# A third score bank for VectorE, and layer 2's FFN spread over the next chunk's attention, in a two-layer transformer kernel

## The chip, the cores and the metric

The kernel runs on one core of one Trainium2 chip. The metric is the device time of one execution in microseconds. The granted clock is the share of TensorE's full clock that the profile records.

## The reference

Two identical layers, each with attention and an FFN, in bfloat16, on one sequence of 2048 rows of 512 columns. There are 32 heads of 16 columns, and the FFN's width is 1792.

```python
x = A_x
for layer in range(2):                       # written out in the reference
    q, k, v = heads(layernorm(x) @ wqkv)     # 32 heads of 16
    p = softmax(q @ k.T / 4)                 # 2048 x 2048 for each head
    x = x + (p @ v) @ wo
    h = gelu(layernorm(x) @ w1 + b1)         # tanh form
    x = x + h @ w2 + b2
```

## The kernel before

A Python scheduler with a clock of its own decides, while the program is built, in which order each engine runs its instructions. Its thread priorities (smaller is more urgent) and conditions are therefore part of the kernel: a changed number reorders the instructions of all engines.

The scores are computed in tiles of 128 keys by 512 queries of one head, each in one PSUM bank. There are 2 x 32 x 16 x 4 = 4096 of them. PSUM's eight banks are laid out so:

```python
SLOTS = ((0, 1, 2), (3, 4))   # the large and the small score slot: exponentials on ScalarE
PVB = 5                       # value products of the running pass (32 columns for each of 4 heads)
MISC = (6, 7)                 # projections, FFN, and spare score tiles for VectorE
DU = 7                        # pattern buffers: 7, in pairs and one half
```

While ScalarE takes the exponential of one slot, PE (TensorE) fills the other. Besides, VectorE takes some tiles and approximates the exponential. It makes a bfloat16 bit pattern with a multiply and an add, and two further passes make three shifted copies. PE then needs four value products for such a tile in place of one, with weighted copies of the values.

```python
def scores(self):
    while True:
        sl = yield ("acq", "s")                  # a free slot
        cells = [...]                            # a tile for each of its banks
        ...
        op = _Op("pe", MM, fns, ...)             # the score matmuls of the slot
        # when the op is placed, tiles for VectorE may be attached in spare banks 7 or 6
        op.late = lambda op, start: self.attach(op, start, cells, extra, free)
        yield op
        for d, b, pair, j in extra:
            yield ("spawn", self.dfirst(pair, j, b), DPRIO)
            if j == 0:
                yield ("spawn", self.dchain(pair), CPRIO)
        ...

def dfirst(self, pair, j, b):                    # VectorE, first pass: from PSUM
    u = self.T["DU"][pair["du"]][:, 0, j, :]
    yield _Op("dve", 0.68, lambda e: e.tensor_scalar(u, self.bank(b), E_SCALE, E_BIAS,
              op0=ALU.mult, op1=ALU.add), reads=["B.%d" % b], writes=[...])
    yield ("rel", "dbank", b)                    # dchain: two more passes for each pair

def exps(self):                                  # ScalarE
    ...
    yield _Op("act", 0.065 + 0.4267 * n, lambda e: e.activation(out=dst, in_=src, func=ACT.Exp, scale=0.25), ...)
    yield ("rel", "s", sl)                       # the slot is free
```

After the last pass of a chunk of 512 queries come the output projection, a layer norm, the FFN and (after layer 1) the projections for layer 2. They run between the attention instructions of the next chunk. `when(l, c, part)` holds a piece back until that share of the next chunk's score tiles is placed.

The softmax here doesn't subtract the row's maximum and nothing guards it: scores larger than these inputs give would overflow.

Of the kernel before, what the change touches and what calls it, by code (L numbers as in the profile page):

```python
# [19 lines left out]
SLOTS = ((0, 1, 2), (3, 4))  # L20
PVB = 5
MISC = (6, 7)
# [5 lines left out]
GP = 2  # L28

DU = 7  # L30
LAST = 450
EARLY = 4
KD = ((4, 5, 6, 7), (0, 1, 2, 12))
NKD = 4
# [5 lines left out]
MID = 1.4  # L40
QUEUE = 4
DPRIO = 9
CPRIO = 16
FPRIO = 1.5
PVP = 2
PTURG = 6
DUURG = 0
BACKLOG = 1.0
DULOW = 1
DWIDE = 2  # L50
RWIDE = 2
# [287 lines left out]
def bass_interleave_layers__mha_block__dense_activation_gelu__prompt_kernel(  # L339
# [15 lines left out]
    with ExitStack() as es:  # L355
# [20 lines left out]
        du = sb([128, DU // 2, 4, 2, 512], U16, "du")  # L376
        T["DU"] = [du[:, i, :, :, :] for i in range(DU // 2)]
        if DU % 2:
# [60 lines left out]
class _Plan:  # L439
# [164 lines left out]
    def projections(self, l, c, prio):  # L604
        T = self.T
        if l == 0:
            def src(dc, t):
                return T["K"][1][:, dc, t * 128:(t + 1) * 128] if t is not None else T["K"][1][:, dc, 512 * c:512 * c + 512]
            skeys = ["XL.%d" % t for t in range(4 * c, 4 * c + 4)]
        else:  # L610
            def src(dc, t):
                return T["XF"][:, dc, (t % 4) * 128:(t % 4) * 128 + 128] if t is not None else T["XF"][:, dc, :]
            skeys = ["XF.%d" % j for j in range(4)]
        ph = self.phase[c]
        units = []
        if l == 1:
            units = [("K", b) for b in range(4)] + [("V", 4 * c + b) for b in range(4)] + [("Q", b) for b in range(4)]
        else:
            for b in range(4):
                units.append(("K", b))  # L620
                if c == 0:
                    units.append(("Q", b))
                units.append(("V", 4 * c + b))
            if c > 0:
                units += [("Q", b) for b in range(4)]
        for j, (kind, i) in enumerate(units):
            p = prio + (0.01 * j if l else 0.5 if kind == "Q" and c > 0 else 0)
            if l:
                yield ("cond", self.when(0, c, 0.52 + 0.024 * j))
            yield ("spawn", self.proj(l, kind, i, c, src, skeys, ph, (kind, l, i, c)), p)  # L630

    def norm(self, l, qc, g, b, part, final):
# [161 lines left out]
    def post(self, l, c):  # L794

        T = self.T
        tiles = range(4 * c, 4 * c + 4)
        yield ("need", ("otn", l, c, 3))
        for t in tiles:
            yield ("spawn", self.wo(l, c, t), 10)  # L800
        for t in tiles:
            yield ("need", ("xready", t, 2 * l + 1))
        self.phase[c] = 2 * l + 1
        xf, xk = lambda t: T["XF"][:, :, (t % 4) * 128:(t % 4) * 128 + 128], lambda t: ["XF.%d" % (t % 4)]
        yield ("spawn", self.ln(c, xf, xk, 11), 11)
        for t in tiles:
            yield ("need", ("lnt", t, 2 * l + 1))
        for p in range(NFC // 2):
            yield ("cond", self.when(l, c, 0.06 + (0.06 if l else 0.055) * p))
            yield ("spawn", self.hpair(l, c, p), 12 + 0.1 * p)  # L810
        if (l, c) != (NL - 1, self.NQ - 1):
            yield ("spawn", self.gelu(l, c), 12)
        for t in tiles:
            yield ("spawn", self.ytile(l, c, t), 13)
        for t in tiles:
            yield ("need", ("xready", t, 2 * l + 2))
        if l == NL - 1:
            return
        self.phase[c] = 2 * l + 2
        yield ("spawn", self.ln(c, xf, xk, 14), 14)  # L820
        for t in tiles:
            yield ("need", ("lnt", t, 2 * l + 2))
        yield from self.projections(l + 1, c, 15)
# [38 lines left out]
    def setup_attention(self):  # L862
        self.pas = self.passes()
        self.alist, self.dlist, self.left, self.pvleft = [], [], [], {}
        self.base, self.span = {}, {}
        n = 0
        for pi, (l, qc, g, kts, part, final) in enumerate(self.pas):
            self.alist.append([(pi, kt, a) for kt in kts if kt not in KD[l] for a in range(4)])
            self.dlist.append([(pi, kt, a) for kt in kts if kt in KD[l] for a in range(4)])
            self.left.append(4 * len(kts))  # L870
            n += 4 * len(kts)
            self.base[(l, qc)] = n
            for a in range(4):
                self.pvleft[(pi, a)] = len(kts)
        self.total, self.scored, self.nd, self.pa, self.pv = n, 0, 0, 0, 0
        for l in range(NL):
            for c in range(self.NQ):
                self.span[(l, c)] = LAST if (l, c) == (0, self.NQ - 1) else 260 if (l, c) == (1, 0) else 512
        self.aq = {k: [] for k in self.pvleft}
        self.dq = {k: [] for k in self.pvleft}  # L880
        self.cap = [2] * (DU // 2) + [1] * (DU % 2) + [2]
        self.lead = [min(pi for pi, p in enumerate(self.pas) if p[0] == l) for l in range(NL)]
        self.duleft, self.open, self.starved, self.lend = {}, None, 0, 2

    def vcopies(self):
# [64 lines left out]
    def take(self, c, free):  # L950
        self.scored += 1
        self.left[c[0]] -= 1
        if self.left[c[0]] == 0:
            free.append(self.s.tokens[("qp", c[0])])

    def attach(self, op, start, cells, extra, free):
        pools = self.s.pools
        used = {c[2] for c in cells}
        if sum(th.op.cost for th in self.s.threads if th.op is not None and th.op.eng == "dve" and th.prio >= 10) > BACKLOG:
            return  # L960
        for home in ("dbank", "misc"):
            for b in list(pools[home]):
                if len(used) == 4 or self.lend == 2 or not (self.open or pools["du"]):
                    return
                if any(self.s.end.get(ev, 0.0) > start + TOL for ev in self.P.deps([], ["B.%d" % b]) if ev[0] != "pe"):
                    continue
                d = self.next_d(used, start)
                if d is None:
                    if self.open:
                        self.open["full"] = True  # L970
                        self.open = None
                    return
                used.add(d[2])
                pools[home].remove(b)
                if self.open is None:
                    self.open = {"du": pools["du"].pop(0), "cells": [], "full": False}
                pair = self.open
                pair["cells"].append(d)
                extra.append((d, b, pair, len(pair["cells"]) - 1))
                if len(pair["cells"]) == self.cap[pair["du"]]:  # L980
                    self.open = None
                f, r = self.score(d, self.s.tokens[("qp", d[0])], b)
                op.fns.append(f)
                op.reads += r
                op.writes.append("B.%d" % b)
                self.take(d, free)
                self.nd += 1

    def scores(self):
        u = 0  # L990
        pools = self.s.pools
        while True:
            sl = yield ("acq", "s")
            cells = []
            for _ in SLOTS[sl]:
                c = self.next_act()
# [6 lines left out]
            fns, reads, writes, free, extra = [], [], [], [], []  # L1003
            for c, b in work:
                l, qc, g = self.pas[c[0]][:3]
                yield ("need", ("qp", c[0]))
                yield ("need", ("K", l, g // 2, c[1] // 4))
                f, r = self.score(c, self.s.tokens[("qp", c[0])], b)
# [1 line left out]
                reads += r  # L1010
                writes.append("B.%d" % b)
                self.take(c, free)
            ahead = 0.065 + 0.4267 * len(SLOTS[1 - sl])
            op = _Op("pe", MM, fns, reads=reads, writes=writes, mode="S", slack=max(SLACK, ahead - LATE))
            op.late = lambda op, start: self.attach(op, start, cells, extra, free)
            yield op
            for d, b, pair, j in extra:
                yield ("spawn", self.dfirst(pair, j, b), DPRIO)
                if j == 0:
                    yield ("spawn", self.dchain(pair), CPRIO)  # L1020
# [11 lines left out]
    def dfirst(self, pair, j, b):  # L1032
        u = self.T["DU"][pair["du"]][:, 0, j, :]
        yield _Op("dve", 0.68, lambda e: e.tensor_scalar(u, self.bank(b), E_SCALE, E_BIAS, op0=ALU.mult, op1=ALU.add),  # L1034
                  reads=["B.%d" % b], writes=["DU.%d.0.%d" % (pair["du"], j)] + self.over(pair["du"]))
        pair["done"] = pair.get("done", 0) + 1
        yield ("rel", "dbank", b)

    def over(self, du):
        return ["K0.%d.%d" % (i, c) for i in (2, 3) for c in range(self.NQ)] if du == len(self.cap) - 1 else []  # L1040
# [46 lines left out]
    def exps(self):  # L1087
        T = self.T
        u = 0
        while True:  # L1090
# [3 lines left out]
            sl, cells = got  # L1094
# [14 lines left out]
            for r, (pi, kt, a) in zip(run, cells):  # L1109
                l, _, g = self.pas[pi][:3]  # L1110
                h = 8 * (g // 2) + 2 * a + (g % 2)
                self.aq[(pi, a)].append((T["V"][l][:, kt, h, 0:17], T["PT"][:, r, :],
                                         ["V%d.%d" % (l, kt), "V%d1" % l, "PT.%d" % r], ("pt", r), True, kt))
            yield ("rel", "s", sl)
            u += 1
        for sl in range(len(SLOTS)):
            yield ("take", ("s", sl))
# [134 lines left out]
```

## Time and profile before

| | |
|---|---|
| median | 1698.77 us (3 runs, 1696.15 to 1699.09; a fourth, later, makes it 1698.42) |
| ScalarE busy | 1597.9 us, 94% |
| VectorE busy | 1251.7 us, 74% |
| PE busy | 1441.1 us, 85% |

The page of the profiled execution. The first line is the span; the second the busy time of each engine; PEclk is the granted TensorE clock in tenths of full speed, in 40 slices (9 is 0.9 or more); the last the shares of the chain of waits.

```profile
span 1700.3 us, 28713 instructions
...
PE 1441.1 (85%) x11935; PEld 370.9 (22%) x11935; DVE 1251.7 (74%) x2377; ACT 1597.9 (94%) x1386; POOL 103.1 (6%) x134
...
PEclk9999999989998999999898999988999899898988
...
ACT 68%; PE 23%; issue 5%; DVE 3%; DMA 1%; POOL 0%; POOLq 0%; SPq 0%
...
```

The groups of instructions, shapes apart: line, engine, operation, shapes and count, then busy time in us and mean ns of one, then the engine's idle time before them and what ended it. The first two lines are the exponentials of the large and of the small slot.

```profile
...
L1106 ACT ACTIVATE pt<-ps 128x1536 bf16<-128x1536 f32 x667 | 1012.3, 1518 | 39.3 <-PE ps L919 25.7 <-PE ps L1165 12.1
L1106 ACT ACTIVATE pt<-ps 128x1024 bf16<-128x1024 f32 x666 | 729.7, 1096 | 6.2 <-PE ps L919 5.4 <-PE ps L1165 0.2
L919 PE MATMUL ps<-qp,kt 32*128 32x512 bf16 x4096 | 549.5, 399 | 175.5 <-ACT pt L1106 152.6 <-DVE du L1034 3.9 <-DVE kt L1034 3.2
...
L1034 DVE TENSOR_SCALAR du<-ps 128x512 uint16<-128x512 f32 x572 | 387.1, 686 | 199.5 <-PE ps L919 192.3 <-PE ps L778 2.3
...
```

Instructions on ScalarE overlap by some 0.15 us, so the mean durations overstate what one costs. The better unit is the time from the end of the predecessor to its own end. In the trace the median of that is 1.344 us for three banks and 0.916 us for two. I call the sum of these units the **exponential work** (667 x 1.344 + 666 x 0.916 + one single bank = 1507.0 us), and everything in which an exponential ends later than that a **stall** (57.1 us). With these two the span closes:

| us, profiled run | before |
|---|---|
| until the first exponential starts | 18.4 |
| exponential work | 1507.0 |
| stalls | 57.1 |
| gelus, table loads, copies between exponentials | 65.8 |
| after the last exponential (the last chunk's FFN) | 52.1 |
| sum | 1700.3 |

Who waited for whom, in total, times and longest in us: ScalarE first, then PE.

```profile
...
ACT pt L1106 <- PE ps L919: 31.0, 55, 2.1
...
ACT pt L1106 <- PE ps L1165: 12.3, 11, 2.7
...
```

```profile
...
PE ps L919 <- ACT pt L1106: 152.6, 305, 1.1
...
PE ps L919 <- DVE du L1034: 3.9, 10, 0.8
...
PE ps L919 <- DVE kt L1034: 3.2, 6, 1.0
...
```

ScalarE waits for score matmuls (L919) and, where no probability buffer is free, for value products (L1165).

### The profile page before, as it was taken

The numbers are of one execution on the slowest core, as the hardware profiler recorded it, in microseconds if no ns is written. First come the engines' busy times: TensorE is split into PE (matmuls) and PEld (weight loads), VectorE is DVE, ScalarE is ACT, GpSimd is POOL, SyncE is SP. The second block draws the span as 40 slices with busy tenths as digits, with TensorE's granted clock in tenths as the row PEclk, the third lists the DMA queues.
The fourth block names the chain that finished last, engine by engine and source line by source line (L and its number), as shares of the span: only waits on it lengthen the run. The fifth ranks groups of instructions, "written<-read, shape, count | busy, mean of one in ns | idle before, by whom it ended". The sixth has DMA issues, their size and how long they took to land.

```text
span 1700.3 us, 28713 instructions
## 1 busy us (share of the span) xinstructions
PE 1441.1 (85%) x11935; PEld 370.9 (22%) x11935; DVE 1251.7 (74%) x2377; ACT 1597.9 (94%) x1386; POOL 103.1 (6%) x134
## 2 busy tenths in 40 slices
PE   7987789888898888899887987789888897898876
PEld 2221122222221222222122221112222221221212
DVE  6478897568885787667776778887678689885861
ACT  6999999999999999999999999998999999999972
POOL 3100010000000000000100010100000000000000
PEclk9999999989998999999898999988999899898988
DMA  6000001001010101101011010001001000110001
GB/s 173 13 1 1 1 13 45 13 20 32 23 41 8 26 26 28 42 1 44 7 38 32 1 44 8 1 13 38 22 23 39 22 11 1 26 38 13 8 13 50
DMA packets 85150, 42.49 MB, mean 25 GB/s; under 512 B 34589, under 2 KB 85022, under 8 KB 85022
## 3 DMA queue, kind: packets, MB, share of 16 engines
q1 hardware_dynamic: 85022, 40.65, 9.0%
q8 instruction: 96, 1.57, 0.4%
q14 instruction: 32, 0.26, 0.1%
HBM read 30.68 MB, written 2.10 MB: 19 GB/s over the span
## 4 chain that ended last, share of the span: by engine, by line
ACT 68%; PE 23%; issue 5%; DVE 3%; DMA 1%; POOL 0%; POOLq 0%; SPq 0%
ACT pt L1106 64%; PE ps L1165 8%; PE ps L919 7%; PE ps L737 3%; ACT g L763 3%; PE ps L776 2%; PE ps L578 2%; DVE du L1034 1%; PE ps L575 1%; DMA xf<-xln 1%; ACT L1106 1%; ACT L763 1%; PE ps L680 1%; DVE du L1059 0%; DVE du L1061 0%
## 5 line engine op out<-in xcount | busy, mean ns | idle before, releaser
L1106 ACT ACTIVATE pt<-ps 128x1536 bf16<-128x1536 f32 (+1 forms) x1334 | 1520.1, 1306 | 45.4 <-PE ps L919 31.0
L919 PE MATMUL ps<-qp,kt 32*128 32x512 bf16 x4096 | 549.5, 399 | 175.5 <-ACT pt L1106 152.6
L1034 DVE TENSOR_SCALAR du<-ps 128x512 uint16<-128x512 f32 x572 | 387.1, 686 | 199.5 <-PE ps L919 192.3
L1165 PE MATMUL ps<-pt,v 128*17 128x512 bf16 x3334 | 468.9, 400 | 5.1 <-DVE xt L653 2.1
L1165 PE MATMUL ps<-du,vc 128*17 128x512 bf16 x1716 | 327.8, 402 | 0.0
L919 PEld LDWEIGHTS ps<-qp,kt 32*128 32x128 bf16 x4096 | 139.7, 91 | 750.2 <-ACT pt L1106 375.3
L1061 DVE TENSOR_SCALAR du<-du 128x2048 uint16<-128x2048 uint16 (+1 forms) x289 | 198.4, 688 | 3.7
L776 PE MATMUL ps<-w,g 128*128 128x512 bf16 x448 | 136.0, 413 | 46.0 <-ACT g L763 46.0
L1165 PE MATMUL ps<-du,v 128*17 128x512 bf16 x572 | 165.0, 403 | 2.6 <-DVE xt L653 1.2
L905 POOL TENSOR_SCALAR qp<-q,mask 128x512 bf16<-128x512 bf16 x84 | 61.3, 730 | 1378.2 <-PE ps L919 1370.1
L737 PE MATMUL ps<-xf,wr 128*128 128x512 bf16 x448 | 123.6, 391 | 15.1 <-DMA xf<-xln 15.0
L1165 PEld LDWEIGHTS ps<-pt,v 128*17 128x17 bf16 x3334 | 89.2, 88 | 164.8 <-issue 136.4
L1059 DVE TENSOR_SCALAR du<-du 128x1024 uint16<-128x1024 uint16 (+1 forms) x289 | 121.7, 423 | 3.8
L1165 PE MATMUL ps<-dh,vc 128*17 128x512 bf16 x300 | 105.7, 413 | 0.0
L1034 DVE TENSOR_SCALAR kt<-ps 128x512 uint16<-128x512 f32 x90 | 61.6, 684 | 39.1 <-PE ps L919 38.5
L1165 PEld LDWEIGHTS ps<-du,vc 128*17 128x17 bf16 x1716 | 73.3, 91 | 68.7 <-issue 45.6
L750 DVE TENSOR_SCALAR g<-ps,hb1t 128x512 bf16<-128x512 f32 x98 | 73.2, 747 | 15.7 <-PE ps L737 14.6
L1034 DVE TENSOR_SCALAR dh<-ps 128x512 uint16<-128x512 f32 x100 | 68.6, 686 | 21.4 <-PE ps L919 20.7
L1165 PE MATMUL ps<-kt,vc 128*17 128x512 bf16 x270 | 71.1, 390 | 0.0
L776 PEld LDWEIGHTS ps<-w,g 128*128 128x128 bf16 x448 | 32.6, 101 | 118.0 <-issue 59.6
L783 DVE TENSOR_TENSOR x<-x,ps 128x512 bf16<-128x512 bf16 x32 | 21.8, 681 | 46.1 <-PE ps L778 38.6
L737 PEld LDWEIGHTS ps<-xf,wr 128*128 128x128 bf16 x448 | 33.4, 99 | 76.6 <-issue 49.6
(70 smaller groups left out, 913.5 us busy)
## 6 DMA issues: line engine op xcount, KB each, us to landing
wr<-in_B_w_dram SPq DMA_DIRECT2D x56, 256.0 KB, 2.8
wr<-in_A_wqkv_dram SPq DMA_DIRECT2D x24, 256.0 KB, 2.7
wr<-in_A_wo_dram SPq DMA_DIRECT2D x16, 256.0 KB, 2.7
x<-in_A_x_dram SPq DMA_DIRECT2D x4, 512.0 KB, 8.9
out_dram<-x SPq DMA_DIRECT2D x16, 128.0 KB, 1.7
w<-in_B_w_dram SPq DMA_DIRECT2D x1, 1792.0 KB, 10.7
g<-in_A_wqkv_dram SPq DMA_DIRECT2D x3, 512.0 KB, 6.5
xf<-xln SPq DMA_TRANSPOSE x48, 2.4
```

What stands on the lines that cost most here:

```text
L578: fns.append(lambda e, dc=dc: e.matmul(pb, lhsT=wt(dc), rhs=src(dc, None), start=(dc == 0), stop=(dc == NDC - 1)))
L737: fns = [lambda e, dc=dc, j=j, pb=pb: e.matmul(pb, lhsT=T["WR"][:, w, 256 * dc + 128 * j:256 * dc + 128 * j + 128], rhs=T["XF"][:, dc, :], ...
L750: yield _Op("dve", 0.74, lambda e, fc=fc, pb=pb: e.tensor_scalar(T["G"][:, fc, :], pb, T["HB1T"][:, fc:fc + 1], None, op0=ALU.add), reads= ...
L763: fns.append(lambda e, g=g: e.activation(out=g, in_=g, func=ACT.Gelu_apprx_tanh))
L776: fns = [lambda e, fc=fc: e.matmul(pb, lhsT=T["G"][:, fc, q], rhs=T["W2"][:, fc, :], start=(fc == 0), stop=False) for fc in range(NFC)]
L905: yield _Op("pool", 0.7, lambda e, s=s, b=b, t=t, qc=qc: e.tensor_scalar(T["QP"][:, s, :], T["Q"][:, b, 512 * qc:512 * qc + 512], T["MASK" ...
L919: return (lambda e: e.matmul(o, lhsT=lhsT, rhs=rhs, start=True, stop=True, tile_position=(32 * a, 0)), ["K%d.%d.%d" % (l, g // 2, kt // 4) ...
L1034: yield _Op("dve", 0.68, lambda e: e.tensor_scalar(u, self.bank(b), E_SCALE, E_BIAS, op0=ALU.mult, op1=ALU.add), reads=["B.%d" % b], write ...
L1059: yield _Op("dve", 0.08 + 0.14 * n, lambda e: e.tensor_scalar(U[:, 1, 0:n, :], U[:, 0, 0:n, :], SHIFT, None, op0=ALU.add), reads=key[0], w ...
L1061: yield _Op("dve", 0.08 + 0.28 * n, lambda e: e.tensor_scalar(U[:, 2:4, 0:n, :], U[:, 0:2, 0:n, :], 2 * SHIFT, None, op0=ALU.add), reads=k ...
L1106: yield _Op("act", 0.065 + 0.4267 * n, lambda e, src=src, dst=dst: e.activation(out=dst, in_=src, func=ACT.Exp, scale=0.25), reads=["B.%d" ...
L1165: op.fns.append(lambda e, o=o, lhsT=lhsT, rhs=rhs, a=a, st=not begun[a], sp=self.pvleft[k] == 0: e.matmul(o, lhsT=lhsT, rhs=rhs, start=st, ...
```

## The change

Its intent is twofold. First, VectorE may also take a tile out of the large slot: when no tile could be attached in a spare bank and VectorE is about free (within `SWAP` = 0.5 us), the slot's third bank gets a VectorE tile, and ScalarE's exponential covers two banks only. The slot becomes free when both engines are done. Second, the FFN of layer 2 is spread over more of the next chunk, and the second FFN matmul (of both layers) and the projections start later in it. Four settings change with it: the priority of layer norms (`LNP`), that of the later VectorE passes (`CPRIO`), the urgency of value products when pattern buffers run out (`DUURG`), and a backlog limit.

```diff
+LNP = 7
+SWAP = 0.5
+HB = (0.05, 0.05)
+HS = (0.05, 0.09)
+YB = (0.4, 0.7)
+YS = (0.05, 0.06)
+JB = 0.64
+JS = 0.025
-CPRIO = 16
+CPRIO = 8
-DUURG = 0
-BACKLOG = 1.0
+DUURG = 1
+BACKLOG = 9
 ...
-                yield ("cond", self.when(0, c, 0.52 + 0.024 * j))       # projections of layer 2
+                yield ("cond", self.when(0, c, JB + JS * j))
 ...
-        yield ("spawn", self.ln(c, xf, xk, 11), 11)                      # the second one was 14
+        yield ("spawn", self.ln(c, xf, xk, LNP), LNP)
 ...
-            yield ("cond", self.when(l, c, 0.06 + (0.06 if l else 0.055) * p))
+            yield ("cond", self.when(l, c, HB[l] + HS[l] * p))
 ...
+            yield ("cond", self.when(l, c, YB[l] + YS[l] * (t % 4)))    # second FFN matmul
             yield ("spawn", self.ytile(l, c, t), 13)
 ...
+    def swap(self, op, start, cells, extra, free):
+        if extra or self.lend == 2 or len(cells) < 3 or not (self.open or self.s.pools["du"]):
+            return
+        if self.s.clock["dve"] > start + SWAP:
+            return
+        ...                                  # the slot's third tile goes back to its queue,
+        self.join(op, d, SLOTS[0][2], extra, free)   # a tile for VectorE takes the bank
 ...
-            ahead = 0.065 + 0.4267 * len(SLOTS[1 - sl])
+            ahead = 0.065 + 0.4267 * self.held[1 - sl]
-            op.late = lambda op, start: self.attach(op, start, cells, extra, free)
+            op.late = lambda op, start: (self.attach(op, start, cells, extra, free), self.swap(op, start, cells, extra, free))
 ...
-            yield ("rel", "s", sl)
+            yield from self.slot_done(sl)    # both users must be done
```

## The prediction

> **What bounds it now.** ScalarE. The page's busy line gives ACT 94% of the span (1598 us), VectorE 74%, PE 85%; the chain of waits is 64% exponentials (L1106). Between 18 and 1648 us ACT runs 667 three-bank and 666 two-bank exponentials nearly back to back. In the trace one ends 1.344 us (three banks) or 0.916 us (two) after its predecessor: 0.428 us a bank and 0.06 us an instruction. Together they need 1507 us; about 57 us more are stalls, 48 of them before a three-bank exponential, when PE had only a short two-bank one in which to refill the large slot. ACT's waits agree (PE scores 31 us; value products, which hold the probability buffers, 12 us). Seven gelus with table loads cost 62 us. The first 18 us and the last 52 us (the last chunk's FFN) are fixed.
>
> **What the change does.** From the instruction order of both programs:
> - VectorE takes 838 score tiles instead of 762. The exponentials become 530 three-bank and 834 two-bank: 712 + 764 = 1476 us, 31 us less. About 137 third banks go over; some 60 ordinary attachments to spare banks are lost, so 76 tiles are net.
> - VectorE: 76 first passes (0.686 us) and their share of the two later passes (1.12 us a pair): about 95 us more, 1252 to about 1345 us, 80% of the shorter span.
> - PE: 228 more value products, in fours 57 rounds of 0.21 us, 12 us. PE has that slack on average.
> - Places with four or more dense matmuls between score groups fall from 165 to 115. At 1100-1200 us, early in layer 2, where ACT stalled about 10 us, there should be less pile-up. Layer 2's last gelu comes later, 139 instead of 226 ScalarE tiles before the end, still in front of the tail.
> - Scores, gelus, table loads and dense matmuls keep their counts.
>
> **On the critical path.** All 31 us are ACT work. Against that: (a) a swapped large slot has a two-bank exponential too, so PE has 0.92 us, not 1.34, to refill the small slot behind it. Applying before's mean stall for each kind of PE work between score groups to the new order, I estimate 62 us of stalls instead of 57. (b) The large slot now needs ACT and VectorE both to finish. VectorE's queue is in order and fuller; where an operation waiting for PE stands ahead, the slot is held and ACT starves: a few us. (c) The smoother FFN returns a few us. Simultaneous reads are of different banks, which the Trainium skill, "PSUM — Partial Sum Buffer", section "PSUM bank collisions raise a hardware error", says run clean; no run here tests it yet.
>
> Net gain about 26 us: **1672 us**, 8 in 10 between 1658 and 1688. Faster by over 2%: 0.25; within 2%: 0.74; slower by over 2%: 0.01.
>
> **What would show it.** Exponential busy time (1520 us) falls to about 1490; VectorE busy about 1340 us; PE's waits for ACT before scores fall, its waits for VectorE's first passes rise from 8 us to 10-25; ACT's waits for PE scores stay at 25-45 us; the tail stays near 52 us; granted clock near 0.93.
>
> **What would make it wrong.** VectorE lagging behind the schedule's assumption: then PE waits tens of us for first passes and the gain vanishes. Layer 2's stalls shrinking by more than (a) and (b) cost: then 1655-1662 us. A denser PE stream lowering the granted clock, value products falling behind: ACT's wait for them well over 12 us.

## More of the kernel before

One run of the kernel before, at 1918.26 us with a mean granted clock of 0.641, was slow. It left no trace and its cause is open.

PE waits for ScalarE much more (152.6 us) than ScalarE for PE. That made PE look as if it had room. The next view shows what this reading misses. It gives, for stretches of the span, the busy us and the instruction counts of each engine, and the granted clock:

```profile
...
core 0: us, PE busy (x) PEld busy (x) DVE busy (x) ACT busy (x) POOL busy (x), PEclk, DMA share, GB/s
658.00:664.00 6.00, 3.90 (x39) 0.90 (x33) 5.58 (x14) 6.00 (x7) 0.01 (x1) 0.98 0.13 26
664.00:667.40 3.40, 3.40 (x29) 0.72 (x27) 0.60 (x1) 2.59 (x3) 0.00 (x0) 0.54 0.19 38
667.40:670.80 3.40, 1.78 (x20) 0.55 (x17) 3.29 (x9) 3.40 (x4) 0.00 (x0) 0.96 0.33 67
670.80:674.20 3.40, 3.40 (x30) 0.66 (x29) 1.42 (x3) 2.50 (x3) 0.00 (x0) 0.53 0.06 13
674.20:690.00 15.80, 15.41 (x127) 4.11 (x120) 13.79 (x26) 15.73 (x15) 0.69 (x1) 1.00 0.12 34
...
```

In the second and fourth stretch, one 3.4 us window each, the clock is near one half. PE is busy from end to end and ScalarE is busy only 2.59 and 2.50 of 3.40 us. In the stretches at full clock ScalarE is busy nearly throughout.

## The result, and the profile after

In the first comparison the changed kernel took 1679.13 us (median of 4 runs, 1676.37 to 1683.28) against 1698.42 us (4 runs), a ratio of 0.9891 with a 95% interval of 0.9867 to 0.9914. Ratios here are the mean time of one kernel's fast runs over that of the other's of the same rounds, so they are not quite the ratio of the medians that I quote. It is 1.1% faster, clear of noise.

The page, the groups and the waits of the changed kernel, the lines that answer to those of before:

```profile
span 1678.4 us, 29283 instructions
...
PE 1440.2 (86%) x12013; PEld 376.7 (22%) x12163; DVE 1322.5 (79%) x2543; ACT 1571.8 (94%) x1416; POOL 108.9 (6%) x134
...
PEclk9999999999999999989989999889899989799898
...
ACT 53%; PE 36%; issue 7%; DVE 4%; DMA 1%; POOL 0%; POOLq 0%; SPq 0%
...
```

```profile
...
L1154 ACT ACTIVATE pt<-ps 128x1024 bf16<-128x1024 f32 x834 | 854.6, 1078 | 17.9 <-PE ps L930 14.5 <-PE ps L1213 2.1
L1154 ACT ACTIVATE pt<-ps 128x1536 bf16<-128x1536 f32 x530 | 795.6, 1501 | 32.4 <-PE ps L930 18.5 <-PE ps L1213 12.3
L930 PE MATMUL ps<-qp,kt 32*128 32x512 bf16 x4096 | 555.4, 397 | 147.6 <-ACT pt L1154 121.9 <-DVE du L1074 5.5 <-DVE mv L519 2.3
...
L1074 DVE TENSOR_SCALAR du<-ps 128x512 uint16<-128x512 f32 x626 | 424.4, 685 | 161.3 <-PE ps L930 154.8
...
```

```profile
...
ACT pt L1154 <- PE ps L930: 32.9, 71, 1.4
...
ACT pt L1154 <- PE ps L1213: 14.4, 12, 6.0
...
```

```profile
...
PE ps L930 <- ACT pt L1154: 121.9, 239, 8.1
...
PE ps L930 <- DVE du L1074: 5.5, 14, 0.9
...
PE ps L930 <- DVE kt L1074: 1.0, 2, 0.8
...
```

The exponentials shift from three banks to two (530 and 834), as the order of the program had said, and their busy time falls from 1520.1 to 1493.9 us. ScalarE still waits as much for PE as before. PE hardly waits for VectorE's first passes (L1074): 5.5 + 1.0 us here against 3.9 + 3.2 us. The account closes again:

| us, profiled runs | before | changed | difference |
|---|---|---|---|
| until the first exponential starts | 18.4 | 19.3 | +0.9 |
| exponential work | 1507.0 | 1476.3 | -30.7 |
| stalls | 57.1 | 66.5 | +9.4 |
| gelus, table loads, copies | 65.8 | 65.8 | 0 |
| after the last exponential | 52.1 | 50.4 | -1.7 |
| sum | 1700.3 | 1678.4 | -21.9 |

So the work went as foreseen, and a third of it came back as stalls. To see whose stalls they are, I took every stalled exponential. I asked which came last for it: a free probability buffer, or the score matmuls of its slot. For the latter, I asked what came last before them: PE's own previous work, ScalarE's release of the slot, or a VectorE pass. The trace has the times of all semaphore updates, so this is a reading of the trace and not of the schedule.

| stalls by what came last, us | before | changed |
|---|---|---|
| PE still in value products | 27.2 | 33.0 |
| PE still in dense matmuls | 16.0 | 14.9 |
| value products late, no probability buffer free | 13.8 | 15.7 |
| ScalarE's release of the slot alone | 0 | 2.0 |
| VectorE's first pass (always of a tile in bank 7) | 0 | 1.0 |
| all | 57.1 | 66.5 |

The largest single stall of the changed kernel is new, 6 us near 1137 us. The timeline there (start us, us, engine, what; in brackets the idle time before it and its releaser):

```profile
...
1125.56 5.54 ACT L1154 ACTIVATE pt<-ps 128x1024 bf16<-128x1024 f32 x5
...
1130.19 0.68 DVE L517 BATCH_NORM_STATS2 stats<-x 128x6 f32<-128x512 bf16 x1
...
1131.21 0.66 DVE L517 BATCH_NORM_STATS2 stats<-x 128x6 f32<-128x512 bf16 x1
...
1132.47 0.66 DVE L517 BATCH_NORM_STATS2 stats<-x 128x6 f32<-128x512 bf16 x1
...
1133.49 0.69 DVE L1109 TENSOR_SCALAR du<-du 128x2048 uint16<-128x2048 uint16 x1
...
1134.71 0.68 DVE L1109 TENSOR_SCALAR du<-du 128x2048 uint16<-128x2048 uint16 x1
1135.31 0.68 DVE L657 TENSOR_TENSOR kt<-kt,ps 128x512 f32<-128x512 f32 x1
...
1136.04 0.12 PEld L1213 LDWEIGHTS ps<-pt,v 128*17 128x17 bf16 x8 [1.70 <-DVE kt L657]
1136.04 1.03 PE L1213 MATMUL ps<-pt,v 128*17 128x512 bf16 x8 [0.78 <-DVE kt L657]
...
1137.13 1.45 ACT L1154 ACTIVATE pt<-ps 128x1536 bf16<-128x1536 f32 x1 [6.03 <-PE ps L1213]
...
```

VectorE runs layer-norm statistics (L517) and later passes (L1109) before it reaches the addition (L657) that frees the value products' bank. PE waits for it, no probability buffer comes free, and ScalarE stands for 6.03 us.

Then there is the clock. In the records of both traces it is either full or one half, and the half-clock spells last multiples of 3.4 us. Those that begin inside the attention (before the last exponential ends) come to 205 us before and 171 us in the changed kernel. (The 184 us in the expectation of e7 counts one more, which begins 10 us after the last exponential.) Of the 57.1 us of stalls before, 38.9 us fall into these spells or the 2 us after them, which are some 16% of the attention; of the changed kernel's 66.5 us, 38.2 us do. So the stalls at full clock rose, from 18.2 to 28.3 us, and those of the half clock stayed about the same. (Two stalls of before, 3.0 us, lie at the very edge of the 2 us; with them the split is 41.9 and 15.2 us.)

What precedes a spell is a window in which PE had less to do. (A window is one stretch of 3.41 us on the grid on which all the spells begin and end.) Before, the 35 such windows had 16.4 matmul starts on average and PE busy for 50% of the time, the other full-clock windows 26.8 starts and 89%. Nearly all of PE's idle time in them, 55.5 of 60 us, ended with a result of ScalarE (exponentials 36.6 us, gelus 18.9 us). The Trainium skill, "TensorE: Matmul & The Clock Gate", section "What's actually happening", says much the same: the slow state is the default, and the clock falls back to it after an idle window of about 3.4 us. This trace agrees on the window and the clock, with spells in multiples of 3.41 us and a clock of 0.5, but most of the windows in front of a spell were not idle: 32 of the 35 had 7 matmul starts or more. There the measurement decides.

### The profile page after: what moved, and what is told of

It reads as the page before. It is cut to its first block, busy times and chain, and to the rows that moved or that the text cites. A ratio compares the mean times of both kernels' runs of the same rounds, so it can differ in the third digit from the quotient of the medians.

```text
span 1678.4 us, 29283 instructions
## 1 busy us (share of the span) xinstructions
PE 1440.2 (86%) x12013; PEld 376.7 (22%) x12163; DVE 1322.5 (79%) x2543; ACT 1571.8 (94%) x1416; POOL 108.9 (6%) x134
## 4 chain that ended last, share of the span: by engine, by line
ACT 53%; PE 36%; issue 7%; DVE 4%; DMA 1%; POOL 0%; POOLq 0%; SPq 0%
ACT pt L1154 50%; PE ps L1213 13%; PE ps L930 11%; PE ps L784 5%; PE ps L745 3%; ACT g L771 2%; PE ps L586 2%; PE ps L583 1%; DVE du L1074 1%; PE ps L688 1%; DVE du L1109 1%; DMA xf<-xln 1%; ACT L771 0%; DVE kt L1074 0%; DVE g L758 0%
## 5 line engine op out<-in xcount | busy, mean ns | idle before, releaser
L1154 ACT ACTIVATE pt<-ps 128x1536 bf16<-128x1536 f32 (+1 forms) x1364 | 1493.9, 1242 | 50.3 <-PE ps L930 32.9
L1074 DVE TENSOR_SCALAR du<-ps 128x512 uint16<-128x512 f32 x626 | 424.4, 685 | 161.3 <-PE ps L930 154.8
L1213 PE MATMUL ps<-du,vc 128*17 128x512 bf16 x1878 | 338.6, 399 | 2.1 <-DVE du L1109 1.1
L1109 DVE TENSOR_SCALAR du<-du 128x2048 uint16<-128x2048 uint16 (+1 forms) x317 | 218.0, 691 | 2.9
L784 PE MATMUL ps<-w,g 128*128 128x512 bf16 x401 | 123.1, 408 | 36.0 <-ACT g L771 29.7
L745 PE MATMUL ps<-xf,wr 128*128 128x512 bf16 x394 | 115.9, 389 | 22.4 <-DMA xf<-xln 13.1
L1107 DVE TENSOR_SCALAR du<-du 128x1024 uint16<-128x1024 uint16 (+1 forms) x317 | 130.2, 417 | 2.7
L1213 PE MATMUL ps<-dh,vc 128*17 128x512 bf16 x339 | 114.3, 395 | 0.0
L1074 DVE TENSOR_SCALAR dh<-ps 128x512 uint16<-128x512 f32 x113 | 77.3, 684 | 29.4 <-PE ps L930 28.2
L1074 DVE TENSOR_SCALAR kt<-ps 128x512 uint16<-128x512 f32 x99 | 67.7, 684 | 32.5 <-PE ps L930 31.5
L1213 PE MATMUL ps<-kt,vc 128*17 128x512 bf16 x297 | 72.3, 405 | 0.0
L1109 DVE TENSOR_SCALAR dh<-dh 128x1024 uint16<-128x1024 uint16 x113 | 47.8, 423 | 1.2
```

What stands on the lines that cost most here:

```text
L745: fns = [lambda e, dc=dc, j=j, pb=pb: e.matmul(pb, lhsT=T["WR"][:, w, 256 * dc + 128 * j:256 * dc + 128 * j + 128], rhs=T["XF"][:, dc, :], ...
L784: fns = [lambda e, fc=fc: e.matmul(pb, lhsT=T["G"][:, fc, q], rhs=T["W2"][:, fc, :], start=(fc == 0), stop=False) for fc in range(NFC)]
L1107: yield _Op("dve", 0.08 + 0.14 * n, lambda e: e.tensor_scalar(U[:, 1, 0:n, :], U[:, 0, 0:n, :], SHIFT, None, op0=ALU.add), reads=key[0], w ...
L1109: yield _Op("dve", 0.08 + 0.28 * n, lambda e: e.tensor_scalar(U[:, 2:4, 0:n, :], U[:, 0:2, 0:n, :], 2 * SHIFT, None, op0=ALU.add), reads=k ...
L1154: yield _Op("act", 0.065 + 0.4267 * n, lambda e, src=src, dst=dst: e.activation(out=dst, in_=src, func=ACT.Exp, scale=0.25), reads=["B.%d" ...
L1213: op.fns.append(lambda e, o=o, lhsT=lhsT, rhs=rhs, a=a, st=not begun[a], sp=self.pvleft[k] == 0: e.matmul(o, lhsT=lhsT, rhs=rhs, start=st, ...
```

## The experiments

I held three theories at first. **A**: time follows the exponential work, and the held large slot costs next to nothing. **B**: the large slot that VectorE still holds starves ScalarE. **C**: the gain comes from the FFN's places and the priorities. Each kernel's exponential work can be counted from its instruction order before it runs, with the units of the first trace. "Parts" are third banks, settings and FFN places.

### e1: third banks alone

```diff
 (the changed kernel with)
-CPRIO = 8;  DUURG = 1;  BACKLOG = 9;   layer norms at LNP = 7
+CPRIO = 16; DUURG = 0;  BACKLOG = 1.0; layer norms at 11 and 14
-HB = (0.05, 0.05); HS = (0.05, 0.09);  YB = (0.4, 0.7);   JB = 0.64; JS = 0.025
+HB = (0.06, 0.06); HS = (0.055, 0.06); YB = (-1.0, -1.0); JB = 0.52; JS = 0.024
```

> The third-bank rule alone, all priorities and FFN places as before. Its order has 789 VectorE tiles (152 of them third banks), and 1498.5 us of exponential work at the unit times of the first trace against 1507.0 before. Theory A (time follows the exponential work; a held large slot costs next to nothing): 5 to 9 us faster, 1690 to 1694 us, PE's waits for first passes under 12 us. Rival B (a large slot that VectorE still holds starves ScalarE, and that ate the missing gain): same or slower than before, PE's waits for first passes over 15 us. Rival C (the gain of the change is the FFN's placing and the priorities): no change within 2 us.

Measured: 1702.36 us (6 runs) against 1701.16 us, ratio 1.0002 (0.9975 to 1.0030). A's time failed, and B's mechanism failed: PE's waits for first passes were 6.2 + 0.7 + 0.2 = 7.1 us. C's forecast of no change came true here; e2 and e3 speak against C. The six runs of this one program reached from 1694.5 us, at a mean clock of 0.947, to 1705.5 us, at 0.930. The profiled run is the fastest of them. The 8.5 us of work are gone by the order of the program, but the interval leaves room for a gain of about 4 us at most.

### e2: the four settings alone

```diff
 (the changed kernel with the FFN places of before, as in e1, and)
-            op.late = lambda op, start: (self.attach(...), self.swap(...))
+            op.late = lambda op, start: self.attach(...)
```

> Only the four settings (layer norm, chain, buffer urgency, backlog), no third banks, FFN places as before. 783 VectorE tiles, 1497.5 us of exponential work, 9.5 us less than before. A: 7 to 11 us faster, 1688 to 1692 us. C: most of the change's 19 us, 1679 to 1684 us.

Measured: 1699.74 us against 1701.16 us, ratio 0.9992 (0.9961 to 1.0023). Both fail. Its profiled run has 9.5 us less exponential work and 9.4 us more stalls (66.5), with a mean clock of 0.927.

### e3: the FFN's places alone

```diff
 (the changed kernel with the settings of before, as in e1, and without swap, as in e2)
```

> Only the places of the FFN and projections. 768 VectorE tiles, 1504.2 us of exponential work, 2.8 us less. A: 1 to 5 us faster, 1694 to 1698 us; ScalarE stalls behind dense matmuls stay near 16 us. C: at least 8 us faster, with stalls behind dense matmuls under 10 us.

Measured: 1711.78 us against 1701.16 us, ratio 1.0058 (1.0033 to 1.0084). It is slower, which neither theory had. The work is 2.8 us less; the stalls are 72.3 us, 15 us more. Stalls behind dense matmuls are 15.9 us, unchanged, and those behind value products rose to 38.3 us. Two lines of its page, to be read against those of before:

```profile
span 1710.1 us, 28632 instructions
...
PEclk9999999989998999999998999788899989898898
...
```

Its half-clock time in the attention is 242 us, and 53.4 us of its stalls lie in or just behind it. C is out in this form: placed so without the rest, the FFN's work costs time.

### e4: layer norm behind the later passes

```diff
-        yield ("spawn", self.ln(c, xf, xk, LNP), LNP)     # both places
+        yield ("spawn", self.ln(c, xf, xk, 11), 11)       # and 14 in the second
```

> The changed kernel with the layer norm's priority put back to 11 and 14, behind the chain passes at 8. 857 VectorE tiles, 1466.9 us of exponential work, 9.4 us less than the changed kernel. A: 1664 to 1672 us, 8 to 14 us under the changed kernel, and the one 6 us stall near 1137 us of the changed kernel, when layer-norm statistics and chain passes stood ahead of the work that frees the value-product bank, is gone. B: VectorE is fuller still, so stalls eat it: 1676 to 1682 us.

Measured: 1778.48 us, and a **wrong result** (relative error 0.35). The order that comes of this setting lets the next chunk overwrite tiles of the attention output before the output projection of the previous chunk is placed; I found 24 such reads by following who wrote each tile in the order of the program. The generator orders what is placed, so it knows no hazard against an operation that it has not placed yet. The time is of no use for the theories either, because the order falls apart around a gelu. ScalarE's waits:

```profile
...
ACT pt L1154 <- PE ps L930: 89.0, 65, 33.4
ACT g L771 <- DVE g L758: 42.8, 1, 42.8
...
```

Whether the 6 us stall comes from the layer norm's higher priority is left open by this. It is in e5, e7 and e11 too (5.8 to 6.0 us) and is 8.1 us in e12; all of these have third banks and the four settings. Kernels with only one of the two (e1, e2, e9, e10) have no stall over 3.2 us anywhere. But one of 5.2 us is in e3, which has neither.

After these four I formed theory **D**: time is start + exponential work + stalls + the rest; the stalls are PE's; and two thirds of those before come from half-clock spells, which PE's idle windows bring about. Its rival **F**: the stalls come from PE's load and not from its clock.

### e5: third banks and settings, FFN places of before

```diff
-HB = (0.05, 0.05); HS = (0.05, 0.09);  YB = (0.4, 0.7);   JB = 0.64; JS = 0.025
+HB = (0.06, 0.06); HS = (0.055, 0.06); YB = (-1.0, -1.0); JB = 0.52; JS = 0.024
```

> Third banks and the four settings, FFN places as before. 827 VectorE tiles, 1480.8 us of exponential work, 26 us less than before. Theory D (the gain is exponential work, which only third banks and settings together bring; ScalarE's stalls stay near 65 us and come from PE, two thirds of them around PE's half-clock spells): 1678 to 1688 us, so the FFN's places give little. Rival C (the FFN's places are what makes it pay): 1692 us or more.

Measured: 1687.13 us against 1701.36 us, ratio 0.9918 (0.9898 to 0.9938). D holds; the stalls of the profiled run are 67.7 us, 40.8 us of them around the half-clock spells. Third banks and settings bring most of it together, though each alone brought nothing. The order of the programs shows why. Third banks alone give 152 third banks but cost 125 of the 762 tiles in spare banks (789 tiles in all). With the settings there are 827. In the full change, putting `DUURG` alone back drops the tiles from 838 to 801: value products that free pattern buffers sooner are what lets VectorE take more. (That last count is of a program built and not run.)

### e6: the third bank held longer

```diff
-        yield _Op("dve", 0.68, lambda e: e.tensor_scalar(u, self.bank(b), ...), ...)
+        hold = lambda e: e.tensor_reduce(out=scr, in_=self.bank(b), axis=X, op=ALU.add)
+        yield _Op("dve", 0.68, [fn] if b in MISC else [hold, fn], ...)    # same order, cost not told
```

> The changed kernel in the same order, but each of the 149 third banks is read twice by VectorE (a sum into a scratch column first), so the large slot is held some 0.7 us longer, about 100 us of VectorE work in all. Theory D: VectorE has the room and the hold is rarely the last to end; under 10 us slower than the changed kernel. Rival B (the hold is near the critical path): 25 us or more slower, with PE waits for first passes over 30 us.

Measured: 1714.89 us against 1701.36 us, ratio 1.0078 (1.0057 to 1.0100), about 32 us above the changed kernel (by the two ratios, 1.0078 / 0.9891; they shared no rounds). D's number failed and B's passed. The added instruction, then PE's waits for first passes, then ScalarE's for score matmuls:

```profile
...
L1078 DVE TENSOR_REDUCE scr<-ps 128x1 f32<-128x512 f32 x149 | 101.6, 682 | 8.7 <-PE ps L931 8.0
...
```

```profile
...
PE ps L931 <- DVE du L1075: 24.3, 67, 0.9
...
PE ps L931 <- DVE kt L1075: 5.8, 13, 1.0
PE ps L931 <- DVE dh L1075: 5.5, 16, 0.8
...
```

```profile
...
ACT pt L1159 <- PE ps L931: 54.3, 124, 1.3
...
```

149 reads of 682 ns, 101.6 us, cost about a third of themselves. Of the stalls, now 99.6 us, 24.4 us end with the pass on the third bank and 6.1 us with one on bank 7; in the changed kernel these were 0 and 1.0. So no stall ends with the hold as it stands, but it has less than 0.7 us of room. The traces show the room directly, when each pass on a third bank is matched to its slot's exponential by the order of the program: in the changed kernel 136 of the 149 passes end first, by 0.65 us at most (median of all 0.33 us); in e6 142 of 149 end after the exponential (median 0.41 us). The experiment also fills VectorE's queue: VectorE begins at the slot 0.2 us later than in the changed kernel (medians). Against the 0.68 us of the second read that is the smaller part of the shift, but the stalls are not split between the two.

### e7 and e8: keeping PE busy

The same orders, but where the scheduler sees PE idle over 0.3 us and a spare bank is free, dummy matmuls fill 0.7 of that gap. They write the spare bank, whose next user starts it anew, so the results stay right.

```diff
+    def warm(self, t, start):                    # called before each PE operation is placed
+        n = int(WARM * (start - t) / MM) if start - t > WGAP else 0     # 0.7 and 0.3
+        ...
+        for b in list(self.s.pools["dbank"]) + list(self.s.pools["misc"]):
+            if ...:                              # the bank's last reader is done
+                fn = lambda e: e.matmul(o, lhsT=w[:, 0, 0:128], rhs=w[:, 1, :], start=True, stop=True)
+                self.P.group("pe", [fn] * n, ["W2"], ["B.%d" % b])
+                return
```

> The changed kernel in the same order, plus 277 dummy matmuls in 109 gaps of PE's queue, into a spare bank, so that PE idles less. D: half-clock time within the attention falls from about 184 us by a third or more, ScalarE's stalls fall by 8 to 20 us, 1660 to 1672 us. Rival F (stalls are PE's load, not its clock): the extra 59 us of PE work make it the same or slower, 1678 us or more.

> The kernel before in the same order, plus 340 dummy matmuls in 124 gaps of PE's queue. D: half-clock time falls from about 205 us by a third or more, stalls by 8 to 20 us, 1680 to 1692 us, so the changed kernel's lead at the warmer clock is 15 to 30 us. F: 1698 us or more.

Measured: the changed kernel with dummies 1668.21 us (5 runs, 1667.21 to 1668.69), ratio to before 0.9803 (0.9782 to 0.9823). The kernel before with dummies 1683.22 us (6 runs, 1678.36 to 1688.32), ratio 0.9895 (0.9872 to 0.9919). Both are faster with more PE work in them, so F is out. The stalls before fell by 21.1 us, just over the range expected. With dummies in both and in the same rounds the changed kernel leads by 15.0 us, of the 30.7 us of work that it saves. Spans and clocks of before with dummies and of the changed with dummies, each followed by ScalarE's waits:

```profile
span 1676.6 us, 29188 instructions
...
PEclk9999999999998999999898999999999999999999
...
```

```profile
...
ACT pt L1111 <- PE ps L924: 15.5, 36, 1.0
...
ACT pt L1111 <- PE ps L1170: 9.8, 11, 2.9
...
```

```profile
span 1665.4 us, 29789 instructions
...
PEclk9999999999999999999999999989999999899899
...
```

```profile
...
ACT pt L1159 <- PE ps L935: 23.0, 53, 1.0
...
ACT pt L1159 <- PE ps L1218: 15.6, 12, 5.8
...
```

| profiled runs, us | half clock in the attention | stalls | of them in half-clock spells or 2 us after | at full clock |
|---|---|---|---|---|
| before | 205 | 57.1 | 38.9 | 18.2 |
| before with dummies (e8) | 75 | 36.0 | 18.0 | 18.0 |
| changed | 171 | 66.5 | 38.2 | 28.3 |
| changed with dummies (e7) | 92 | 55.7 | 20.5 | 35.2 |

In both kernels the stalls of the half-clock spells about halve. Were they due to the work that falls there, they would have come back at full clock; before's at full clock stay (or rise by 3 us, with the two stalls at the edge of the 2 us). The changed kernel's rise by 7 us, but 5.9 us of that is the one large stall, which VectorE brings about: in the changed kernel it happens to lie in a half-clock spell, in e7 at full clock. Without it the stalls go from 32.0 to 20.5 us around the spells and from 28.3 to 29.3 us at full clock. (e8's profiled run is its fastest; its median lies 5 us higher.)

### e9 to e12: the parts at the warmer clock

All four are e7 with one thing changed in the source: e9 without `swap`, e10 with the settings of before, e11 with the FFN places of before (the rule then places 279, 358 and 286 dummies, counted by building them, in place of 277), and e12 with

```diff
-WARM = 0.7
-WGAP = 0.3
+WARM = 0.9
+WGAP = 0.22
```

> The changed kernel with the dummy matmuls, but without third banks: settings and FFN places stay. 782 VectorE tiles, 1498.0 us of exponential work (1476.3 with third banks). Its order lets one tile of the attention output be overwritten before its output projection is queued, so the result should be wrong; only the time is wanted. Theory D (at the warmer clock the third banks gain 22 us of work and give back 10 to 15 us of stalls): 1674 to 1682 us against the 1668 us of the same kernel with third banks. Rival G (the stalls that third banks bring eat their whole gain): 1670 us or less.

> The changed kernel with the dummy matmuls, but with the four settings of before. 803 VectorE tiles, 1492.3 us of exponential work. D: 16 us more work than the 1668 us kernel, so 1678 to 1688 us. Rival (settings matter only for the order of small work): 1672 us or less.

> The changed kernel with the dummy matmuls, but with the FFN's places of before. 827 VectorE tiles, 1480.8 us of exponential work, 4.5 us more. D: 1670 to 1676 us. Rival C (the FFN's places matter beyond the tiles): 1680 us or more.

> The changed kernel with 401 dummy matmuls instead of 277, filling 0.9 of the gaps instead of 0.7 and smaller gaps too. D: half-clock time within the attention at or under the 92 us of the 277, 1662 to 1669 us. Rival F (PE's load): slower than 1670 us because less room is left for PE to catch up.

All in one set of rounds, against before at 1702.86 us:

| | median us | ratio to before (95%) | exponential work | stalls (profiled) |
|---|---|---|---|---|
| e9, no third banks | 1682.12 | 0.9886 (0.9853 to 0.9919) | 1498.0 | 49.8 |
| e10, old settings | 1672.14 | 0.9825 (0.9798 to 0.9853) | 1492.3 | 44.2 |
| e11, old FFN places | 1669.18 | 0.9805 (0.9778 to 0.9831) | 1480.8 | 48.7 |
| e12, more dummies | 1668.95 | 0.9806 (0.9779 to 0.9832) | 1476.3 | 55.9 |

e9's result was wrong (relative error 0.06), as expected. G is out: e12, with all parts and in the same rounds, is 13 us faster, so the third banks give back some 9 of their 22 us of work (e12 has more dummies than e9, but they make no difference between e7 and e12). e9's time lies just above D's range, and e11's just below. e10 missed D by 6 us: against e12 the settings bring 16 us of work but only 3 us of time here. Part of that is the clock again: e10, with the most dummies but e12, has the least half-clock time of all, 51 us against 75 us in e12. With the FFN places the difference is 0.2 us. e12 has its half-clock time down from 92 to 75 us and is no faster than e7: its stalls around the half-clock spells are 16.1 us in place of 20.5 us, and those at full clock 39.8 us in place of 35.2 us. Half of that rise is the one large stall, 8.1 us for 5.8 us. So more dummies bring nothing further here.

## Why the prediction was right or wrong

The time was right: 1672 us predicted, 1658 to 1688 as the range, 1679.13 us measured, within 2%. Of the net gain of 26 us, 19 us came. Part of that is luck: the prediction knew nothing of the half clock, and the stalls around the half-clock spells happened to be alike in the two profiled runs (38.9 and 38.2 us). In the other orders without dummies (e1, e2, e3, e5) they reach from 32.9 to 53.4 us, a range as wide as the gain.

- **ScalarE bounds it; 31 us of exponential work go.** Right to a tenth: 30.7 us in the account, and the exponentials' busy time fell to 1493.9 us (about 1490 predicted).
- **VectorE about 1340 us.** 1322.5 us. The direction is right, and it is no bound.
- **(a) PE has less time to refill, 62 us of stalls.** This is the term that was mis-sized: 66.5 us in the profiled run. Its path is in the trace, and at about its size: the two-bank exponentials of the small slot behind a swapped large slot stalled 40 ns each (6.1 us in 154), those of the small slot before 13 ns (8.5 us in 659), which makes some 4 us more. What the estimate lacked lies elsewhere, because it put the mean stalls of before onto the new order: small slots behind an ordinary three-bank exponential stalled 15.7 us in 523, 30 ns each, and 12.9 us of that is in or just behind half-clock spells. By what came last, the 10.1 us more at full clock are 5.2 us behind value products, 3.4 us behind dense matmuls, and the rest behind releases and first passes.
- **(b) The large slot held by VectorE, a few us; waits for first passes 10 to 25 us.** Wrong as a cost: 1.0 us of stalls, none of them at a third bank, and PE's waits stayed near 7 us. Right as a danger: e6 shows that the hold has less than 0.7 us of room. The Trainium skill, "PSUM — Partial Sum Buffer", "PSUM bank collisions raise a hardware error", says that engines reading different banks run clean. The runs agree: ScalarE on banks 0 and 1 and VectorE on bank 2 of one slot, 149 times in an execution, with correct results.
- **(c) The smoother FFN returns a few us; less pile-up at 1100-1200 us.** Not shown. Stalls behind dense matmuls fell by 1.1 us, and the new 6 us stall lies in that very stretch. Alone the FFN's places cost 10 us (e3); with dummy matmuls they are worth 0.2 us (e11 against e12); without dummies and with the other parts e5 and the changed kernel lie 5 us apart by their ratios and 8 us by their medians, but they are of different rounds and the intervals (0.9898 to 0.9938, 0.9867 to 0.9914) overlap.
- **"PE has that slack on average."** This was the wrong picture. PE's idle time is not free here: windows with PE idle for half of the time came before the half-clock spells, and what PE then lacks stalls ScalarE. e8 shows it on the kernel before alone: more PE work, 18 us less time.
- **"The granted clock stays near 0.93."** 0.945. It also moves from run to run, and the time with it: the eleven runs of before in one set reached from 1695.9 us at 0.940 to 1706.9 us at 0.932. That spread is as large as the effects looked for in e1 and e2, which is why e7's runs, within 1.5 us of each other, were the better place to compare. The prediction's risk that a denser PE stream lowers the clock went the other way: with dummies the granted clock is 0.972 (e7) and 0.978 (e8).

The third banks make the stalls at full clock larger: without dummies they are 26.6 to 28.3 us in the profiled runs that have third banks (e1, e5 and the changed kernel) and 15 to 19 us in those that have none (before, e2, e3). In the changed kernel 8.4 us of them lie at the swapped slots and at the small slots behind them. Left open are by which way the third banks do it (the shorter exponentials or the further value products, which no run parts), and whether the layer norm's priority brings the 6 us stall.

The best version is the changed kernel with dummy matmuls (e7): 1668.21 us, ratio 0.9803 to before (0.9782 to 0.9823, by the 2% rule unclear). It beats both kernels. From the two ratios it is about 0.9% under the changed kernel (0.9803 / 0.9891), with which it shared no rounds.

## What to carry to other kernels

Split the span of the bounding engine into work, which can be counted from the program, and stalls, and ask of each stall what came last; a change that takes work off the bounding engine usually pays part of it back there. An engine that waits a lot is not thereby free: look at the granted clock beside its idle time, because here windows with TensorE half idle were followed by matmuls at half clock, and 277 dummy matmuls were worth about 1% of the time. Where a generated order is tuned by many numbers, parts tested alone can come out at zero or negative and still pay together, and every new order has to be checked for its result.

## What the Trainium skill lacked or had wrong

- "TensorE: Matmul & The Clock Gate", "What's actually happening", ties the half clock to an idle window, and "HAM oscillation — how this bites in real kernels" gives as a rule no PE gaps over about 3.4 us. Here windows with work in them also lead to it: before, the full-clock windows in front of a spell had 16.4 matmul starts on average against 26.8 in the others, and 19 of the 35 had 18 to 22 starts, nearly all of 32-row or 17-column tiles. "A second HAM failure mode: psum-queue depth-cycling" on that page does tell of short idle times that are enough, but no passage gives a share of activity below which the clock falls, and these runs do not fix one either.
- The same page tells of gaps from DMA waits and from cycling through PSUM banks. Here the gaps are PE waiting for ScalarE (55.5 of 60 us in the windows in front of a spell), which is the engine that bounds the kernel. They recur through the whole span: 205 us at half clock inside the attention, and 18 us (1.1%) of the time came back in e8.
- No page that I read says that dummy matmuls in a spare PSUM bank can be worth their cost on a kernel bound by another engine: 1701.36 to 1683.22 us before (the same rounds), 1679.13 to 1668.21 us changed (different rounds).
